# Attention scores by 64-row halves of the matmul array, three products instead of four

## The chip, the cores and the metric

The kernel runs on one core of a Trainium2 chip. Its engines work side by side, each through its own list of instructions in order: TensorE (PE; its weight loads are listed apart as PEld), VectorE (DVE), ScalarE (ACT), GpSimd (POOL) and SyncE (SP), which here issues nearly all DMA transfers. The metric is the device time of one execution, in microseconds; the time of a kernel is the median of several runs. TensorE's clock has two levels, 1.2 and 2.4 GHz; the profile shows the granted one as 0.50 and 1.00.

## The reference

Four batches, eight heads, 576 positions, head dimension 64. Attention with a bias that depends on position alone, then a mixing along the sequence, then a two-layer network over 512 channels, all in float32:

```
scores = q @ k.T / 8 + bias(i, j)         # bias: 1 -> 32 -> 8 heads, from log1p(|i-j|) / log1p(max(i,1))
attn   = exp(scores - max); attn /= sum + 1e-9
x      = (attn @ v)  as [4, 576, 512]
h      = x.T @ U @ V                       # along the sequence, rank 32
u      = x + h.T
out    = u + relu(u @ w_ch1) @ w_ch2       # 512 -> 2048 -> 512
```

## The kernel before

Attention goes by pairs of heads: 16 pairs (`p`), each in nine slots (`s`). 576 query rows are four blocks of 128 and 64 left over. Slot 0 does the leftover rows of both heads of the pair in one tile of 128; slots 1 to 8 do the four blocks of the two heads in turn. A slot's scores are a 128x576 tile in two PSUM banks of 288 keys each (`ps`, line 323).

To keep float32 accuracy with the faster `float32r` type, q and k are split into a high part and a rest. `raw` holds a pair's q and k, loaded twice so that both 64-row halves of the partitions hold the same 64 dimensions. `prep_ops` (lines 145 to 170) writes `hi` (high parts; for q the upper 64 partitions are then overwritten with the rest, line 163) and `lo` (the rest of k). A matmul over 128 partitions with q's high part and rest stacked as weights, against k's high part on both halves, gives two of the products; the same weights against k's rest give the other two. So each half of the keys takes two matmuls of 128x288 (line 343), four per slot, with a weight load each. In slot 0 each head's leftover queries stand beside zeros (64 columns of padding), and the two heads are added up: eight matmuls.

For pair 0 `prep_ops` runs early on ACT and DVE, inside the loop that builds the bias; for the others it runs on POOL, in slots 2 to 5 of the pair before. `raw` has one buffer: the load of pair p+2 (`load_pair`, lines 132 to 138, issued in slot 7) waits until POOL has finished with pair p+1. `hi` and `lo` have two.

The order of the work is the order in which the code issues it. `slot` (line 513) issues a slot's scores first, then transposes (lines 411, 419, 428, 465, 467) of tiles that earlier slots have finished, the exponentials on ACT, and in slots 2 and 8 the products with v (line 447, tile `o`). DVE adds the bias and takes the row maximum (line 345) straight from PSUM. So PE goes, in most slots, from scores to transposes and on to the next scores. Transposes and scores work on the whole array (128x128); `o` works on 128x64 column tiles, two of them side by side; `mt` (line 486), once per batch, on 128x32 column tiles, its last part on 64x32. Between 345 us and the end there is only the network (lines 592 and 615), which the change doesn't touch except for the width of a tile.

Of the kernel before, what the change touches and what calls it, by code (L numbers as in the profile page):

```python
# [8 lines left out]
F32 = mybir.dt.float32  # L9
F32R = mybir.dt.float32r  # L10
# [4 lines left out]
ALU = mybir.AluOpType  # L15
# [3 lines left out]
B, H, S, D = 4, 8, 576, 64  # L19
HP = H // 2  # L20
DM = H * D
# [4 lines left out]
P = 128  # L26
HALF = S // 2
LEFT = S - 4 * P
K0 = 2 * S + LEFT
QKW = 2 * K0  # L30

LINE = 16
NTAB = 2 * S - 1
# [15 lines left out]
def kernel(  # L49
# [13 lines left out]
):  # L63
    nc = tc.nc
    mm = nc.tensor.matmul

    def halves(ap):
        return ap.rearrange("p (a b) -> p a b", a=2)
# [6 lines left out]
    p0 = ExitStack()  # L75
# [9 lines left out]
    qkp = ctx.enter_context(tc.tile_pool(name="qkp", bufs=2, side="left"))  # L85
# [27 lines left out]
    rawp = p1.enter_context(tc.tile_pool(name="rawp", bufs=1, side="left"))  # L113
# [5 lines left out]
    qk_ops = {}  # L119
    v_t = {}  # L120

    def pair_loads(p):

        b, hp = divmod(p, HP)

        def part(lo, a, e):
            if p not in qk_ops:
                qk_ops[p] = rawp.tile([P, QKW], F32, tag="raw", name="raw")
            nc.sync.dma_start(out=qk_ops[p][lo : lo + D, a:e], in_=qk[b, hp, :, a:e])

        return [lambda: part(0, 0, QKW), lambda: part(D, LEFT, QKW), lambda: part(D, 0, LEFT)]

    def load_pair(p):
        b, hp = divmod(p, HP)
        raw = rawp.tile([P, QKW], F32, tag="raw", name="raw")
        nc.sync.dma_start(out=raw[0:D], in_=qk[b, hp])
        nc.sync.dma_start(out=raw[D:P], in_=qk[b, hp])
        qk_ops[p] = raw

    def load_v(p):  # L140
        b, hp = divmod(p, HP)
# [3 lines left out]
    def prep_ops(p, early=False):  # L145


        hi = qkp.tile([P, QKW], F32R, tag="hi", name="hi")
        lo = qkp.tile([P, K0 + 2 * LINE], F32R, tag="lo", name="lo")[:, LINE : LINE + K0]
# [11 lines left out]
        def low(out, a, e, p0):  # L161
            eng = nc.vector if early else nc.gpsimd
            eng.tensor_tensor(out=out, in0=raw[p0:P, a:e], in1=hi[p0:P, a:e].bitcast(F32), op=ALU.subtract)  # L163

        return [
            lambda: high(0, K0),
            lambda: low(hi[D:P, 0:K0], 0, K0, D),
            lambda: high(K0, QKW),
            lambda: low(lo, K0, QKW, 0),
        ]  # L170

# [53 lines left out]
    for g in range(4):  # L225
        r = slice(g * HID, (g + 1) * HID)
# [91 lines left out]
    def scores(p, s):  # L318
        d = pair[p]
        hi, lo = qk_ops[p]  # L320
        hp = p % HP
        st = d["st"]
        ps = psum("s", [P, 2, 512], "sc")
        if s == 0:
            terms = [(4 * P, 0), (S, S + LEFT)]
            dst = pmp.tile([P, S], F32, tag="praw", name="praw")
            d["praw"] = dst
        else:
            c, hd = divmod(s - 1, 2)
            if hd == 0:  # L330
                terms = [(c * P, 0)]
                d["P"][c] = pp.tile([P, 2 * S], F32, tag="p", name="p")
                dst = d["P"][c][:, 0:S]
            else:
                terms = [(S + 2 * LEFT + c * P, S)]
                dst = d["P"][c][:, S : 2 * S]
        for a in range(2):
            n = 2 * len(terms)
            i = 0
            for q0, k0 in terms:  # L340
                k1 = k0 + a * HALF
                for kk in (hi[:, K0 + k1 : K0 + k1 + HALF], lo[:, k1 : k1 + HALF]):
                    mm(ps[:, a, 0:HALF], lhsT=hi[:, q0 : q0 + P], rhs=kk, start=(i == 0), stop=(i == n - 1))  # L343
                    i += 1
        nc.vector.tensor_tensor_reduce(  # L345
            out=halves(dst),
            in0=ps[:, :, 0:HALF],
            in1=halves(bias[hp][:, s * S : (s + 1) * S]),
            scale=-0.125,
            scalar=3.0e38,  # L350
            op0=ALU.add,
            op1=ALU.min,
            accum_out=st[:, s : s + 1],
        )
        d["dst"] = dst
# [189 lines left out]

    KD = DM // P
    TB = 256
    NB = NT // TB  # L550
    TT = TB // P
    NG = 4
# [2 lines left out]
    UT = KD * TB  # L555

    acc, uth, utl, wq, hh, hl = {}, {}, {}, {}, {}, {}
# [22 lines left out]
    def mlp1(n):  # L580

        g, j = divmod(n, NB)
        st = {}

        def step(f):
            if f == 0:
                st["ps"] = psum("s", [P, FG, TB], "ph")
            i = 0
            for k in range(KD):
                wh, wl = (w[:, k, f * P : (f + 1) * P] for w in wq[g][0:2])  # L590
                for w, u in ((wh, uth[j]), (wh, utl[j]), (wl, uth[j])):
                    mm(st["ps"][:, f, :], lhsT=w, rhs=u[:, k, :], start=(i == 0), stop=(i == 3 * KD - 1))  # L592
                    i += 1
            if f == FG - 1:
                t = qkp.tile([P, QKW], F32R, tag="hi", name="hh")
# [94 lines left out]
    for i in range(len(order) + 2):  # L690
        if i < len(order):
            bias_hid(order[i])
        if i >= 2:
            bias_mm(order[i - 2])
            bias_out(order[i - 2])
        if i == 9:
            loads += bias_loads(4, 0)
        if i >= 16 and (i - 16) % 8 == 0:
            loads += bias_loads((i - 16) // 8, 0)
        if i in (28, 30):  # L700
            loads += bias_loads({28: 4, 30: 0}[i], 1)
# [107 lines left out]
    t = [qkp.tile([P, K0 + 2 * LINE], F32R, tag="lo", name="ut") for _ in range(2)]  # L809
# [140 lines left out]
```

## Time and profile before

| what | value |
|---|---|
| median of 3 runs | 775.45 us (773.51 to 777.46) |
| the profiled execution | 771.65 us |
| its span, first to last instruction | 769.8 us |
| PE busy | 740.3 us, 96% of the span |
| DVE, ACT, POOL busy | 56%, 46%, 30% |
| chain that ended last | PE 74%, POOL 7%, DMA 6%, DVE 6%, ACT 4% |
| TensorE clock | 1.00 but for two stretches of 3.4 us |

The page shows three stages: until about 56 us the bias is built (DVE and ACT full, DMA near full), until about 345 us attention runs with the conversion of weights in the background, and then the network to the end. A matmul's listed time includes its way through the array, so consecutive ones overlap: how long PE is taken by one is read from the distance between starts, not from the listed time.

### The profile page before, as it was taken

The page shows a single profiled execution, that of the slowest core. Times are in us where ns is not written, and L with a number is a line of the kernel's source. Part 1 is how long each engine was busy: PE and PEld are TensorE (multiplying, and loading weights), DVE is VectorE, ACT ScalarE, POOL GpSimd, SP SyncE. Part 2 cuts the span into 40 slices and gives each one's busy share as a digit, 9 for nine tenths or more (in the row PEclk, how much of TensorE's full clock was granted, in tenths as well). Part 3 has the DMA queues.
Part 4 walks back from the last instruction along what each step waited for, and adds up shares of the span by engine and source line. Part 5 has one row for each costly group of instructions (what it writes and reads, how often), then busy time and mean ns, then how long its engine had stood idle before and what let it go on. Part 6 is the DMA issues. An engine that isn't in the chain of part 4 may idle for free.

```text
span 769.8 us, 13411 instructions
## 1 busy us (share of the span) xinstructions
PE 740.3 (96%) x5132; PEld 612.0 (80%) x5132; DVE 431.4 (56%) x953; ACT 354.4 (46%) x827; POOL 234.3 (30%) x222
## 2 busy tenths in 40 slices
PE   6888899999999999999999999999999999999998
PEld 4326787778768777779789889988998999899986
DVE  7984478868867876662448734762247722221222
ACT  6995677678767676863025513431114410111010
POOL 0004446656664566710015502540015500000000
PEclk9999999999999999999999999999999999999999
DMA  6898994564455547530153301320002200001111
GB/s 200 262 340 265 241 274 112 138 165 124 124 171 138 123 97 209 160 129 2 38 189 110 96 1 42 96 83 1 1 27 84 69 1 1 1 29 55 55 42 69
DMA packets 39423, 83.97 MB, mean 109 GB/s; under 512 B 6976, under 2 KB 9536, under 8 KB 37312
## 3 DMA queue, kind: packets, MB, share of 16 engines
q1 hardware_dynamic: 39120, 82.86, 37.1%
q8 instruction: 41, 0.67, 0.4%
q10 hardware_dynamic: 240, 0.26, 0.1%
q14 instruction: 22, 0.18, 0.1%
HBM read 60.67 MB, written 22.43 MB: 108 GB/s over the span
## 4 chain that ended last, share of the span: by engine, by line
PE 74%; POOL 7%; DMA 6%; DVE 6%; ACT 4%; issue 2%; SPq 1%; DVEq 0%; POOLq 0%; ACTq 0%
PE po L615 24%; PE ph L592 24%; PE o L447 8%; PE sc L343 7%; PE tb L411 5%; DMA raw<-in_qk_dram 4%; DVE ring L260 2%; POOL lo L163 2%; POOL hi L163 2%; POOL hi L157 2%; PE mt L486 1%; DVE wt L207 1%; ACT p L364 1%; PE bs L270 1%; PE tm L419 1%
## 5 line engine op out<-in xcount | busy, mean ns | idle before, releaser
L597 ACT ACTIVATE hh<-ph 128x1024 fp32r<-128x1024 f32 x36 | 36.9, 1026 | 207.6 <-PE ph L592 207.6
L598 DVE SCALAR_TENSOR_TENSOR hh<-ph,hh 128x1024 fp32r<-128x1024 f32 x36 | 44.1, 1224 | 141.2 <-ACT hh L597 141.2
L212 POOL TENSOR_TENSOR wy<-wt,wy 128x256 int32<-128x256 int32 (+1 forms) x68 | 50.2, 739 | 218.7 <-DVE wt L207 198.0
L364 ACT ACTIVATE p<-p,st 128x576 f32<-128x576 f32 x128 | 100.0, 782 | 34.9 <-DVE st L345 34.8
L345 DVE CUSTOM_DVE_ANT_0 p<-sc,bias 128x576 f32<-128x576 f32 x128 | 95.9, 749 | 33.3 <-PE sc L343 26.2
L343 PE MATMUL sc<-hi 128*128 128x288 f32 x320 | 101.8, 334 | 2.0 <-DVE st L345 2.0
L615 PE MATMUL po<-w2q,hh 128*128 128x512 f32 x432 | 101.7, 390 | 1.8 <-DVE acc L618 1.8
L615 PE MATMUL po<-wq,hh 128*128 128x512 f32 x432 | 103.2, 395 | 0.0
L343 PE MATMUL sc<-lo,hi 128*128 128x288 f32 x320 | 90.7, 299 | 3.9 <-POOL lo L163 3.8
L615 PEld LDWEIGHTS po<-w2q,hh 128*128 128x128 f32 x432 | 79.9, 188 | 18.1 <-issue 2.0
L592 PE MATMUL ph<-ut,w1q 128*128 128x256 f32 x768 | 94.2, 280 | 0.0
L615 PEld LDWEIGHTS po<-wq,hh 128*128 128x128 f32 x432 | 80.1, 188 | 17.6
L592 PEld LDWEIGHTS ph<-ut,w1q 128*128 128x128 f32 x768 | 92.1, 188 | 2.1 <-issue 1.2
L447 PE MATMUL o<-pt,v 128*64 128x320 f32 (+1 forms) x640 | 91.2, 412 | 0.9 <-ACT pt L391 0.9
L592 PEld LDWEIGHTS ph<-ut,wq 128*128 128x128 f32 x768 | 90.3, 188 | 1.4
L592 PE MATMUL ph<-ut,wq 128*128 128x256 f32 x768 | 90.6, 277 | 0.0
L618 DVE TENSOR_TENSOR acc<-po,acc 128x512 f32<-128x512 f32 x72 | 49.6, 690 | 73.1 <-PE po L615 73.1
L411 PE MATMUL tb<-ident,p 128*128 128x128 f32 x512 | 77.8, 275 | 3.9 <-DVE x_sb L393 2.5
L343 PEld LDWEIGHTS sc<-hi 128*128 128x128 f32 x320 | 60.9, 190 | 19.2 <-issue 11.6
L447 PEld LDWEIGHTS o<-pt,v 128*64 128x64 f32 x640 | 45.2, 136 | 35.9 <-ACT pt L391 5.5
L157 POOL TENSOR_SCALAR hi<-raw 128x1216 fp32r<-128x1216 f32 x30 | 36.9, 1231 | 105.7 <-DMA raw<-in_qk_dram 90.3
L411 PEld LDWEIGHTS tb<-ident,p 128*128 128x128 f32 x512 | 61.9, 141 | 5.9 <-ACT p L364 2.5
(94 smaller groups left out, 1037.0 us busy)
## 6 DMA issues: line engine op xcount, KB each, us to landing
raw<-in_qk_dram SPq DMA_DIRECT2D x31, 608.0 KB, 7.6
wraw<-in_w_ch_dram SPq DMA_DIRECT2D x64, 256.0 KB, 2.7
bias_dram<-ring SPq DMA_DIRECT2D x26, 295.5 KB, 4.2
v<-in_vp_dram SPq DMA_DIRECT2D x16, 320.0 KB, 8.2
bias<-bias_dram SPq DMA_DIRECT2D x16, 288.0 KB, 4.6
acc<-u_dram SPq DMA_DIRECT2D x18, 256.0 KB, 4.8
out_dram<-acc SPq DMA_DIRECT2D x18, 256.0 KB, 2.0
bias<-bias_dram SPq DMA_DIRECT2D x16, 256.0 KB, 4.7
```

The costliest lines, as they stand in the source:

```text
L157: nc.gpsimd.tensor_scalar(out=hi[:, a:e], in0=raw[:, a:e], scalar1=1.0, scalar2=0.0, op0=ALU.mult, op1=ALU.add)
L212: nc.gpsimd.tensor_tensor(out=st["y"], in0=st["t"], in1=st["y"], op=ALU.add)
L343: mm(ps[:, a, 0:HALF], lhsT=hi[:, q0 : q0 + P], rhs=kk, start=(i == 0), stop=(i == n - 1))
L345: nc.vector.tensor_tensor_reduce(out=halves(dst), in0=ps[:, :, 0:HALF], in1=halves(bias[hp][:, s * S : (s + 1) * S]), scale=-0.125, scalar ...
L364: nc.scalar.activation(out=dst, in_=dst, func=AF.Exp, bias=st[:, s : s + 1], scale=-1.0, accum_out=st[:, 10 + s : 11 + s])
L411: nc.tensor.transpose(bank[:, kb, :], src[:, b0 + kb * P : b0 + (kb + 1) * P], ident)
L447: mm(o[hd * D : (hd + 1) * D, 0:n], lhsT=v[:, vb * D : (vb + 1) * D], rhs=pt[:, pb, :], start=(j == 0), stop=(j == 4),)
L592: mm(st["ps"][:, f, :], lhsT=w, rhs=u[:, k, :], start=(i == 0), stop=(i == 3 * KD - 1))
L597: nc.scalar.activation(out=hh[n], in_=st["ps"], func=AF.Relu)
L598: nc.vector.scalar_tensor_tensor(out=hl[n], in0=st["ps"], scalar=0.0, in1=hh[n].bitcast(F32), op0=ALU.max, op1=ALU.subtract)
L615: mm(ps, lhsT=h, rhs=w, start=(m == 0), stop=(m == 3 * FG - 1))
L618: nc.vector.tensor_tensor(out=a, in0=ps, in1=a, op=ALU.add)
```

## The change

Scores are now made with weights of 64 rows. The lower 64 partitions hold q and the first 288 keys, the upper 64 hold q again and the last 288 keys. High part and rest lie in two tiles of the same layout, `hi` and `lo`, and three products are made: high by high, high by rest, rest by high; rest by rest is left out. Each product is two matmuls, one on each 64-row half of the array, into the two PSUM banks. A slot takes six matmuls of 64x128 weights by 288 columns. Slot 0 makes all 128 leftover rows against the second head's keys, and then the first 64 rows again, against the first head's keys, with 64x64 weights: twelve matmuls; the zero padding is no longer read. A pair's load is six transfers of 917 KB together, formerly two of 1,245 KB together; pair 1's, formerly three with the last at step 32 of the bias loop, has its four key pieces at steps 32 to 35. Conversions are four of 128x896.

```diff
-QKW = 2 * K0
+KA = HALF
+KB = LEFT + HALF
+QQ = 2 * S
+QKW = QQ + KA + KB
...
+        def q(lo):
+            nc.sync.dma_start(
+                out=raw(lo, 0, QQ).rearrange("d (t n) -> d t n", t=2),
+                in_=src[:, 0 : 2 * (S + LEFT)].rearrange("d (t n) -> d t n", t=2)[:, :, 0:S],
+            )
+        def k(lo, to, n, a):
+            nc.sync.dma_start(out=raw(lo, to, n), in_=src[:, a : a + n])
+        return [
+            lambda: q(0),
+            lambda: q(D),
+            lambda: k(0, QQ, KA, K0),
+            lambda: k(D, QQ, KA, K0 + KA),
+            lambda: k(0, QQ + KA, KB, K0 + S),
+            lambda: k(D, QQ + KA, KB, 2 * K0 - KB),
+        ]
...
-            lambda: high(0, K0),
-            lambda: low(hi[D:P, 0:K0], 0, K0, D),
-            lambda: high(K0, QKW),
-            lambda: low(lo, K0, QKW, 0),
+        m = QKW // 2
+        return [lambda: high(0, m), lambda: low(0, m), lambda: high(m, QKW), lambda: low(m, QKW)]
...
-            terms = [(4 * P, 0), (S, S + LEFT)]
+            parts = [(4 * P, P, QQ + KA + LEFT), (4 * P, D, QQ)]
...
-        for a in range(2):
-            n = 2 * len(terms)
-            i = 0
-            for q0, k0 in terms:
-                k1 = k0 + a * HALF
-                for kk in (hi[:, K0 + k1 : K0 + k1 + HALF], lo[:, k1 : k1 + HALF]):
-                    mm(ps[:, a, 0:HALF], lhsT=hi[:, q0 : q0 + P], rhs=kk, start=(i == 0), stop=(i == n - 1))
-                    i += 1
+        terms = ((hi, hi), (hi, lo), (lo, hi))
+        for q0, n, k0 in parts:
+            for i, (q, k) in enumerate(terms):
+                for a in range(2):
+                    r = slice(a * D, (a + 1) * D)
+                    mm(
+                        ps[0:n, a, 0:HALF], lhsT=q[r, q0 : q0 + n], rhs=k[r, k0 : k0 + HALF],
+                        start=(i == 0), stop=(i == len(terms) - 1),
+                    )
...
-        if i in (14, 18, 32):
+        if i in (14, 18, 32, 33, 34, 35):
```

PE's list in pair 1, from the transposes of slot 0 to those of slot 1. Before (`sc` scores, `tb` and `ti` transposes):

```order
L411 MATMUL tb<-ident,p 128x128 x4
L343 MATMUL sc<-hi 128x288
L343 MATMUL sc<-lo,hi 128x288
L343 MATMUL sc<-hi 128x288
L343 MATMUL sc<-lo,hi 128x288
L411 MATMUL tb<-ident,p 128x128 x4
L428 MATMUL ti<-ident,p 128x128 x2
```

The same place in the list after the change:

```order
L429 MATMUL tb<-ident,p 128x128 x4
L359 MATMUL sc<-hi 128x288 x2
L359 MATMUL sc<-lo,hi 128x288 x2
L359 MATMUL sc<-hi,lo 128x288 x2
L429 MATMUL tb<-ident,p 128x128 x4
L446 MATMUL ti<-ident,p 128x128 x2
```

Four score matmuls of the whole array became three twos of 64-row weights (the order gives the rows of the output, 128), between the same transposes.

PE's list from the product with v at the end of pair 0 to the first transposes of pair 1, slot 0 of pair 1 between them. Before:

```order
L447 MATMUL o<-pt,v 64x320 x10
L343 MATMUL sc<-hi 128x288
L343 MATMUL sc<-lo,hi 128x288
L343 MATMUL sc<-hi 128x288
L343 MATMUL sc<-lo,hi 128x288
L343 MATMUL sc<-hi 128x288
L343 MATMUL sc<-lo,hi 128x288
L343 MATMUL sc<-hi 128x288
L343 MATMUL sc<-lo,hi 128x288
L411 MATMUL tb<-ident,p 128x128 x4
```

The same place in the list after the change:

```order
L465 MATMUL o<-pt,v 64x320 x10
L359 MATMUL sc<-hi 128x288 x2
L359 MATMUL sc<-lo,hi 128x288 x2
L359 MATMUL sc<-hi,lo 128x288 x2
L359 MATMUL sc<-hi 64x288 x2
L359 MATMUL sc<-lo,hi 64x288 x2
L359 MATMUL sc<-hi,lo 64x288 x2
L429 MATMUL tb<-ident,p 128x128 x4
```

Eight matmuls became two groups of six, the second with 64 columns of weights.

POOL's list for one pair, the leftover rows' scaling (`pm`) and the conversion of the next pair. Before:

```order
L384 TENSOR_SCALAR pm<-praw,st 128x576
L384 TENSOR_SCALAR pm<-praw,st 128x64
L157 TENSOR_SCALAR hi<-raw 128x1216
L163 TENSOR_TENSOR hi<-raw,hi 64x1216
L157 TENSOR_SCALAR hi<-raw 128x1216
L163 TENSOR_TENSOR lo<-raw,hi 128x1216
```

The same place in the list after the change:

```order
L402 TENSOR_SCALAR pm<-praw,st 128x576
L402 TENSOR_SCALAR pm<-praw,st 128x64
L178 TENSOR_SCALAR hi<-raw 128x896
L184 TENSOR_TENSOR lo<-raw,hi 128x896
L178 TENSOR_SCALAR hi<-raw 128x896
L184 TENSOR_TENSOR lo<-raw,hi 128x896
```

The number of instructions stays, each conversion is over 896 columns, and all are over 128 partitions.

## Rows read from the trace of the kernel before

**Rows 1.** The page, its engines (part 1) and its chain (part 4).

```profile
PE 740.3 (96%) x5132; PEld 612.0 (80%) x5132; DVE 431.4 (56%) x953; ACT 354.4 (46%) x827; POOL 234.3 (30%) x222
...
PE 74%; POOL 7%; DMA 6%; DVE 6%; ACT 4%; issue 2%; SPq 1%; DVEq 0%; POOLq 0%; ACTq 0%
```

**Rows 2.** The view by stretches: length, then busy us (instructions) per engine, clock, DMA.

```profile
30.00:56.00 26.00, 21.09 (x176) 7.26 (x174) 24.60 (x75) 25.14 (x62) 0.00 (x0) 0.93 0.98 333
...
89.20:92.60 3.40, 3.40 (x17) 3.37 (x16) 0.99 (x4) 1.07 (x2) 0.00 (x0) 0.50 0.85 184
...
125.00:175.00 50.00, 49.19 (x361) 38.84 (x361) 38.22 (x101) 36.24 (x93) 28.78 (x25) 1.00 0.60 154
345.00:770.00 425.00, 418.97 (x2732) 376.59 (x2728) 176.79 (x282) 99.01 (x204) 70.80 (x96) 1.00 0.15 49
```

**Rows 3.** Waits of PE from 56 to 345 us: us, times, longest.

```profile
PE sc L343 <- POOL lo L163: 3.8, 3, 2.2
...
PE tx L465 <- DVE w2q L568: 0.2, 1, 0.2
```

**Rows 4.** PE in order of time, 253.5 to 255.9: start, us, line, form, [idle before].

```profile
253.28 0.44 PE L447 MATMUL o<-pt,v 128*64 128x320 f32 x2
253.65 0.40 PE L343 MATMUL sc<-hi 128*128 128x288 f32 x1
253.88 0.29 PE L343 MATMUL sc<-lo,hi 128*128 128x288 f32 x1
...
254.67 0.30 PE L343 MATMUL sc<-lo,hi 128*128 128x288 f32 x1
254.81 0.60 PE L411 MATMUL tb<-ident,p 128*128 128x128 f32 x4
...
255.38 0.30 PE L343 MATMUL sc<-lo,hi 128*128 128x288 f32 x1
...
255.80 0.33 PE L411 MATMUL tb<-ident,p 128*128 128x128 f32 x1
```

**Rows 5.** PE's weight loads (PEld) of the same stretch.

```profile
253.64 0.19 PEld L343 LDWEIGHTS sc<-hi 128*128 128x128 f32 x1 [0.49 <-issue]
...
255.13 0.19 PEld L343 LDWEIGHTS sc<-hi 128*128 128x128 f32 x1
```

**Rows 6.** PE in order of time, 250 to 254, the groups ahead of those.

```profile
250.27 0.60 PE L411 MATMUL tb<-ident,p 128*128 128x128 f32 x4
250.80 2.91 PE L447 MATMUL o<-pt,v 128*64 128x320 f32 x20
```

**Rows 7.** PEld, 141.55 to 144.0, the mixing product's two tile shapes.

```profile
141.59 0.16 PEld L486 LDWEIGHTS mt<-x_sb,u_sb 128*32 128x32 f32 x8 [0.49 <-DVE x_sb L470]
142.59 0.14 PEld L486 LDWEIGHTS mt<-x_sb,u_sb 64*32 64x32 f32 x2 [0.84 <-issue]
```

**Rows 8.** PE, 114.5 to 115.5, transposes of two tile shapes.

```profile
114.65 0.38 PE L465 MATMUL tx<-ident,ot 128*128 128x128 f32 x2
114.87 0.27 PE L467 MATMUL tx<-ident,ot 128*64 128x128 f32 x1
114.97 0.60 PE L411 MATMUL tb<-ident,p 128*128 128x128 f32 x4
```

**Rows 9.** POOL's groups by form: busy us, mean ns, idle before.

```profile
L163 POOL TENSOR_TENSOR lo<-raw,hi 128x1216 fp32r<-128x1216 f32 x15 | 42.3, 2817 | 1.1
L163 POOL TENSOR_TENSOR hi<-raw,hi 64x1216 fp32r<-64x1216 f32 x15 | 42.0, 2801 | 1.2
L157 POOL TENSOR_SCALAR hi<-raw 128x1216 fp32r<-128x1216 f32 x30 | 36.9, 1231 | 105.7 <-DMA raw<-in_qk_dram 90.3 <-PE sc L343 7.0 <-PE tb L411 6.9
```

**Rows 10.** PE, 86.2 to 89.8, pair 2's second matmul.

```profile
88.86 0.40 PE L343 MATMUL sc<-lo,hi 128*128 128x288 f32 x1 [2.16 <-POOL lo L163]
```

**Rows 11.** DMA issues: KB each, median us to landing.

```profile
raw<-in_qk_dram SPq DMA_DIRECT2D x31, 608.0 KB, 7.6
```

**Rows 12.** SP's list, 86 to 91 us, the first load after that wait.

```profile
88.83 0.48 SPq L136 DMA_DIRECT2D raw<-in_qk_dram  x1
```

More of the change, by code (lines that the diff above doesn't have):

```diff
@@ L65 @@
     mm = nc.tensor.matmul
+    KD = DM // P
+    TB = 256
     def halves(ap):
@@ L124, in pair_loads, with raw @@
         b, hp = divmod(p, HP)
-        def part(lo, a, e):
+        src = qk[b, hp]
+        def raw(lo, to, n):
             if p not in qk_ops:
                 qk_ops[p] = rawp.tile([P, QKW], F32, tag="raw", name="raw")
-            nc.sync.dma_start(out=qk_ops[p][lo : lo + D, a:e], in_=qk[b, hp, :, a:e])
-        return [lambda: part(0, 0, QKW), lambda: part(D, LEFT, QKW), lambda: part(D, 0, LEFT)]
-    def load_pair(p):
[L134 to L138, printed above, removed]
+            return qk_ops[p][lo : lo + D, to : to + n]
+        def q(lo):
[13 more added lines that the diff above has]
+        ]
+    def load_pair(p):
+        for o in pair_loads(p):
+            o()
     def load_v(p):
@@ L145, in prep_ops @@
     def prep_ops(p, early=False):
-        hi = qkp.tile([P, QKW], F32R, tag="hi", name="hi")
-        lo = qkp.tile([P, K0 + 2 * LINE], F32R, tag="lo", name="lo")[:, LINE : LINE + K0]
+        hi = qkp.tile([P, 2 * KD * TB], F32R, tag="hi", name="hi")
+        lo = qkp.tile([P, QKW], F32R, tag="lo", name="lo")
         raw = qk_ops[p]
@@ L159, in high, with low @@
                 )
-        def low(out, a, e, p0):
+        def low(a, e):
             eng = nc.vector if early else nc.gpsimd
-            eng.tensor_tensor(out=out, in0=raw[p0:P, a:e], in1=hi[p0:P, a:e].bitcast(F32), op=ALU.subtract)
-        return [
-            lambda: high(0, K0),
-            lambda: low(hi[D:P, 0:K0], 0, K0, D),
-            lambda: high(K0, QKW),
-            lambda: low(lo, K0, QKW, 0),
-        ]
+            eng.tensor_tensor(out=lo[:, a:e], in0=raw[:, a:e], in1=hi[:, a:e].bitcast(F32), op=ALU.subtract)
+        m = QKW // 2
+        return [lambda: high(0, m), lambda: low(0, m), lambda: high(m, QKW), lambda: low(m, QKW)]
     def conv_ops(src, n, finish):
@@ L330, in scores @@
             if hd == 0:
-                terms = [(c * P, 0)]
+                parts = [(c * P, P, QQ)]
                 d["P"][c] = pp.tile([P, 2 * S], F32, tag="p", name="p")
@@ L334, in scores @@
             else:
-                terms = [(S + 2 * LEFT + c * P, S)]
+                parts = [(S + LEFT + c * P, P, QQ + KA)]
                 dst = d["P"][c][:, S : 2 * S]
-        for a in range(2):
-            n = 2 * len(terms)
-            i = 0
-            for q0, k0 in terms:
-                k1 = k0 + a * HALF
-                for kk in (hi[:, K0 + k1 : K0 + k1 + HALF], lo[:, k1 : k1 + HALF]):
-                    mm(ps[:, a, 0:HALF], lhsT=hi[:, q0 : q0 + P], rhs=kk, start=(i == 0), stop=(i == n - 1))
-                    i += 1
+        terms = ((hi, hi), (hi, lo), (lo, hi))
[7 more added lines that the diff above has]
+                    )
         nc.vector.tensor_tensor_reduce(
@@ L543, in slot @@
             av(p, 0)
-    KD = DM // P
-    TB = 256
     NB = NT // TB
@@ L594, in step @@
             if f == FG - 1:
-                t = qkp.tile([P, QKW], F32R, tag="hi", name="hh")
+                t = qkp.tile([P, 2 * UT], F32R, tag="hi", name="hh")
                 hh[n], hl[n] = (t[:, a * UT : (a + 1) * UT].rearrange("p (f t) -> p f t", f=FG) for a in range(2))
@@ L808 @@
     uth[1], utl[1], uth[2], utl[2], uth[3] = big_views(t, [(LINE, None)] + [(UT, KD)] * 5)
-    t = [qkp.tile([P, K0 + 2 * LINE], F32R, tag="lo", name="ut") for _ in range(2)]
+    t = [qkp.tile([P, QKW], F32R, tag="lo", name="ut") for _ in range(2)]
     utl[3], uth[4] = (x[:, LINE : LINE + UT].rearrange("p (k f) -> p k f", k=KD) for x in t)
```

## The prediction

> **What bounds the kernel now.** I read the page's engine part first: PE is busy 96% of the span, the next engine 56%, and the chain that ended last lies on PE for 74% [rows 1]. A busy PE is not yet a bound, since overlapping matmuls count as busy, so I went on to the stretches. In the network (345 us to the end) PE is busy 418.97 of 425 us; nothing the change does reaches there. In attention, 125 to 175 us stands for the rest: PE 49.19 of 50, DVE 38.22, ACT 36.24, POOL 28.78. Only the bias stage is different: at 30 to 56 us DVE and ACT are busy 24.60 and 25.14 of 26 and the DMA engines 0.98, PE less [rows 2]. The list of waits agrees: from 56 to 345 us PE waited for another engine 11.4 us in all (eight rows, the first and the last shown), and 3.8 of them for POOL's conversion of the next pair [rows 3]. So in attention PE's own time decides, and any microsecond put on it or taken off counts nearly in full; at most 11.4 us can come from waits that go away. The chain's 7% on POOL and 6% on DMA say that load and conversion are nearly as late as PE, not that they hold it up for long.
>
> **What a group of scores costs now.** Between the first and the last matmul rows of slot 3, the starts 253.88 and 254.67 are six matmuls apart: 0.132 us each. Coming from transposes costs nothing more: from the first of four transposes (254.81) to the second score matmul (255.38) is 0.57 = 4 x 0.109 + 0.132; the weight load at 255.13 began ahead of its turn and shows no idle time. Nor does going back to transposes: 254.67 to 254.81 is 0.14 [rows 4, 5]. So a usual slot holds PE for 4 x 0.132 = 0.53 us and slot 0 for 1.06.
>
> **Turns saved.** If the two halves of the array work side by side, a two of matmuls takes one turn of 0.132. The rows show it for column tiles: the last two `o` matmuls stand as one row of 0.44, both started at 253.28, and 20 such matmuls last only 2.91 [rows 4, 6]. For row halves no row shows it; I take it over. Then slots 1 to 8 go from four turns to three and slot 0 from eight to six: 10 turns a pair, 160 in all, 21.1 us saved.
>
> **Boundaries added.** Every change of the array's shape shows a price in this trace. (1) Whole array to `o`: the four transposes begin at 250.27, their turns end at 250.27 + 4 x 0.109 = 250.71, `o` begins at 250.80: 0.09 empty [rows 6]. (2) `o` to scores: nine twos lie between 250.80 and 253.28, so the last has its turn until about 253.28 + 0.27 = 253.55; the scores' weight load begins only at 253.64, with idle time put to "issue": again 0.09, and then the load itself is exposed, as the second matmul comes 0.23 after the first (253.65, 253.88) and not 0.13: 0.10 more [rows 4, 5]. (3) Rows alone: `mt` goes from 128x32 to 64x32 tiles, and that load waits 0.84 us although nothing it needs is late [rows 7]. A load into a transpose exposes less: the transposes that start at 255.80, whose load was not ahead of time, have a first row of 0.33 [rows 4] against 0.27 [rows 8]: 0.06. So I price entering a group of 64-row scores from transposes at 0.09 + 0.11 = 0.20 and leaving it at 0.09 + 0.06 = 0.15. Both stand on PE, with nothing beside them.
>
> The Trainium skill has this as a rule: "TensorEngine Tiling (Array Packing)", section "Key Properties", says that changing the tiling mode drains TensorE, while going from one tile to another in the same mode does not. The rows at (1) to (3) agree with it; those of [rows 8] do not, on their face, and make a rival below.
>
> **The sum on PE, per pair.** Slots 1, 4, 5, 6, 7 and 8 stand between transposes: -0.13 + 0.35 = +0.22 each, 1.32. Slot 2 is followed by `o`, where the boundary exists already: -0.13 + 0.20 = +0.07. Slot 3 follows `o`: -0.13 + 0.15 = +0.02. Slot 0 follows `o` too, saves two turns, changes from 64x128 to 64x64 weights in its middle (0.09 + 0.06 for half as many columns) and goes on to transposes: -0.26 + 0.15 + 0.15 = +0.04. Together +1.45, for 16 pairs 23.2; pair 0's slots 0 to 2 stand between bias matmuls of another shape, in the stage that DVE and ACT bound, and drop out: about -0.3. So +22.9 us.
>
> **What is given back.** POOL's conversion of a pair is 2 x 1.23 + 2 x 2.81 = 8.1 us [rows 9]; over 896 of 1216 columns 6.0 (the op over 64 partitions took as long as that over 128, so the wider one costs nothing). The load falls from 1,245 to 917 KB, at 7.6 us to landing per transfer of 608 KB [rows 11]. Load and conversion are thus some 3 to 4 us earlier per pair while PE is 1.4 later: I take POOL's 3.8 us of waits as gone. The longest, 2.16 us at 88.86 [rows 10], is followed by 3.4 us at half clock [rows 2], which held some 1.7 us of work at full clock; I give back 1.5. Of the other 7.6 us, waits for DVE and ACT, a slower PE lets part vanish: between none and all, I take half, 3.8. Sum 9.1. Four more transfers per pair, at 0.48 us each [rows 12], cost SP about 2 us; SP issues in slot 7 for a pair whose conversion starts two slots into the next, and that cover of several slots is shorter only where the DMA engines are near full (until 95 us). There pair 1's key pieces are issued up to three steps later than the last piece before, but the first half of its conversion, all of q, can be done by then, so half of POOL's work is no longer behind that landing. If the cover fails, a wait of the size of the old 2.16 stays: the lower give-back, 5.
>
> **Forecast.** +22.9 - 9.1 = +13.8 on the profiled 771.65: 785.5. The median of the runs is 3.8 above that execution, so 789 in its terms. Bounds of the likeliest case: turns of 0.120 (288 columns at one a cycle of 2.4 GHz) give 480 x 0.012 = 5.8 less, all 11.4 us of waits gone 3.8 less; the give-back of 5, 4 more. Its own range is 780 to 797.
>
> **Rivals.** (A) No boundary between the whole array and row halves. For it: one transpose in a 128x64 shape stands between whole-array ones at 114.87, 0.11 after the second of the two that begin at 114.65, and the next follow at 114.97 without a gap [rows 8]; and all changes with a price but one also change the number type. Against it: that one, `mt`, changes rows alone. Then 21.1 us are saved, POOL's waits and the half clock give 5, and DVE and ACT, busy three quarters of the time, return a part as new waits, say 5 to 10: 775.45 - 19 = 756 (748 to 764). (B) A boundary of 0.09 each way, but with loads pulled ahead, since the other half's weights don't stand in the way: usual slots -0.13 + 0.18 = +0.05, per pair 0.3 - 0.04 - 0.04 - 0.08 = +0.14, 2 us in all, less 9 given back: 768. Against it is the load at 253.64, which began only after the gap. (C) The halves don't run side by side. If only their weight loads queue up, a two takes 2 x 0.11 = 0.21: 480 x 0.08 = 38 more, 827; it decides as soon as the second load of a two has to wait for the first. If the matmuls themselves do, 480 x 0.132 = 63 more, 852. For it: no 64-row twos anywhere in the trace; against it the `o` matmuls. The change would then not do what it says. "TensorE: Matmul & The Clock Gate", section "LDWEIGHTS (loading the stationary operand)" of the Trainium skill, puts a load at its columns over 1.2 GHz whatever the rows: 107 ns by that rule, an estimate for each of the two halves, and the exposed 0.10 agrees.
>
> **How the numbers follow.** The forecast 0.58, A 0.20, B 0.10, C 0.12. The range of 750 to 806 takes in the forecast with its edges, B and most of A; C and the better end of A, under 0.2 together, stay outside. What a measurement of this kernel tells from no change is about 0.5%, 4 us. Faster: A, most of B and a corner of the forecast, 0.28. Same: 0.07. Slower: 0.65.
>
> **What would show it.** In the trace after: two score matmuls starting within 0.01 us of each other (else C); the next two 0.13 later; the first weight load of a group 0.09 after the last transposes' turn, with idle time put to "issue", and a first two that takes 0.1 longer (without these, A or B); the distance between the first transposes of neighbouring slots 0.2 longer; PE's wait for POOL `lo` gone and no half clock near 89 us; conversions of 0.9 and 2.1 us on POOL. A time under 771 makes the boundary price wrong, one over 806 the side-by-side assumption.

## The result: 0.6% slower, and the profile after

| | before | changed |
|---|---|---|
| median, 20 runs each | 773.8 us | 777.97 us |
| lowest to highest | 769.78 to 777.71 | 777.10 to 779.79 |
| ratio | 1 | 1.0057 (95%: 1.0042 to 1.0071) |
| profiled execution's span | 769.8 us | 776.0 us |
| start of the first to start of the last product with v that closes a pair (after slot 8) | 279.8 us | 288.0 us |
| from there to the end | 425.7 us | 423.8 us |

The changed kernel is slower by 4.2 us; 789 had been forecast. Times of before lie far apart, those of the changed kernel close together; the profiled execution of before was one of its fast ones.

First the page of the changed kernel, the engines of part 1 and from part 6 the load of q (as [rows 1] and [rows 11]; the keys' pieces are rows of their own):

```profile
PE 751.6 (97%) x5452; PEld 593.7 (77%) x5452; DVE 437.2 (56%) x953; ACT 355.2 (46%) x827; POOL 204.2 (26%) x222
...
raw<-in_qk_dram SPq DMA_DIRECT2D x32, 288.0 KB, 4.6
```

The view by stretches, as in [rows 2]:

```profile
30.00:56.00 26.00, 20.01 (x180) 6.88 (x182) 25.79 (x71) 24.44 (x59) 3.14 (x2) 0.93 0.97 318
125.00:175.00 50.00, 49.63 (x395) 33.80 (x393) 37.01 (x95) 35.08 (x91) 25.48 (x25) 1.00 0.38 110
352.00:776.00 424.00, 419.50 (x2739) 376.65 (x2737) 177.52 (x283) 99.90 (x206) 70.84 (x96) 1.00 0.15 50
```

PE has more work in the same 50 us (49.19 busy before, 49.63 now), POOL and the DMA engines less. The bias stage and the network are nearly as they were.

What PE does around the scores, in order of time, in the changed kernel (as [rows 4]):

```profile
251.72 0.40 PE L359 MATMUL sc<-hi 64*128 64x288 f32 x2
251.96 0.29 PE L359 MATMUL sc<-lo,hi 64*128 64x288 f32 x2
252.09 0.29 PE L359 MATMUL sc<-hi,lo 64*128 64x288 f32 x2
252.32 0.65 PE L429 MATMUL tb<-ident,p 128*128 128x128 f32 x4
252.81 0.38 PE L446 MATMUL ti<-ident,p 128*128 128x128 f32 x2
253.03 0.27 PE L449 MATMUL ti<-ident,pm 128*128 128x128 f32 x1
253.23 0.40 PE L359 MATMUL sc<-hi 64*128 64x288 f32 x2
```

PE again, in slot 0 of another pair, where the weights narrow to 64 columns:

```profile
180.58 0.40 PE L359 MATMUL sc<-hi 64*128 64x288 f32 x2
180.82 0.30 PE L359 MATMUL sc<-lo,hi 64*128 64x288 f32 x2
180.96 0.29 PE L359 MATMUL sc<-hi,lo 64*128 64x288 f32 x2
181.09 0.29 PE L359 MATMUL sc<-hi 64*64 64x288 f32 x2
181.22 0.29 PE L359 MATMUL sc<-lo,hi 64*64 64x288 f32 x2
181.36 0.29 PE L359 MATMUL sc<-hi,lo 64*64 64x288 f32 x2
181.58 0.66 PE L429 MATMUL tb<-ident,p 128*128 128x128 f32 x4
```

PE's weight loads beside the first of these blocks, at its two boundaries (as [rows 5]):

```profile
252.31 0.42 PEld L429 LDWEIGHTS tb<-ident,p 128*128 128x128 f32 x4 [0.16 <-issue]
...
253.23 0.18 PEld L359 LDWEIGHTS sc<-hi 64*128 64x128 f32 x2 [0.17 <-issue]
```

A two stands as one row: its matmuls start 3 to 4 ns apart, and the next two follows 0.13 later (251.96 to 252.09). So the halves run side by side. The transpose at 253.03 has its turn until 253.14, the scores' load begins at 253.23: 0.09 empty. The second two comes 0.24 after the first and not 0.13: 0.10 of exposed load. On the way back the last turn ends at 252.09 + 0.13 = 252.22, the transposes begin at 252.32, and from the first four to `ti` it is 0.49 = 4 x 0.109 + 0.055. So entering costs 0.20 and leaving 0.15, as priced. But the change from 64x128 to 64x64 weights within slot 0 costs nothing: 180.96 to 181.09 is a plain turn.

### The profile page after: what moved, and what is told of

It is laid out like the page before. It is cut to its first block, busy times and chain, and to the rows that moved or that the text cites. A ratio compares the mean times of both kernels' runs of the same rounds, so it can differ in the third digit from the quotient of the medians.

```text
span 776.0 us, 14159 instructions
## 1 busy us (share of the span) xinstructions
PE 751.6 (97%) x5452; PEld 593.7 (77%) x5452; DVE 437.2 (56%) x953; ACT 355.2 (46%) x827; POOL 204.2 (26%) x222
## 4 chain that ended last, share of the span: by engine, by line
PE 78%; ACT 8%; DVE 8%; DMA 3%; issue 2%; POOL 1%; SPq 1%; ACTq 0%; DVEq 0%; POOLq 0%
PE po L631 24%; PE ph L608 23%; PE o L465 8%; PE sc L359 8%; PE tb L429 6%; PE bs L287 3%; DVE wt L218 2%; ACT p L382 2%; ACT pt L409 1%; DVE p L363 1%; PE tm L437 1%; PE mt L504 1%; DVE wt L212 1%; PE tx L483 1%; ACT ring L275 1%
## 5 line engine op out<-in xcount | busy, mean ns | idle before, releaser
L631 PEld LDWEIGHTS po<-w2q,hh 128*128 128x128 f32 x432 | 79.9, 188 | 16.7 <-issue 0.6
L465 PE MATMUL o<-pt,v 128*64 128x320 f32 (+1 forms) x640 | 88.7, 411 | 0.6 <-ACT pt L409 0.6
L429 PE MATMUL tb<-ident,p 128*128 128x128 f32 x512 | 82.2, 283 | 3.4 <-DVE x_sb L411 1.8
L465 PEld LDWEIGHTS o<-pt,v 128*64 128x64 f32 x640 | 50.8, 136 | 27.6 <-issue 3.0
L429 PEld LDWEIGHTS tb<-ident,p 128*128 128x128 f32 x512 | 55.0, 140 | 20.9 <-issue 11.7
L409 ACT COPY pt<-tb 128x512 f32<-128x512 f32 x88 | 50.9, 579 | 30.4 <-PE tb L429 30.2
L359 PE MATMUL sc<-hi 64*128 64x288 f32 (+1 forms) x320 | 62.4, 386 | 1.9 <-DVE st L363 1.8
L184 POOL TENSOR_TENSOR lo<-raw,hi 128x896 fp32r<-128x896 f32 x30 | 63.2, 2108 | 2.2
L359 PEld LDWEIGHTS sc<-hi 64*128 64x128 f32 (+1 forms) x320 | 29.0, 178 | 40.0 <-issue 32.1
## 6 DMA issues: line engine op xcount, KB each, us to landing
raw<-in_qk_dram SPq DMA_DIRECT2D x32, 288.0 KB, 4.6
bias<-bias_dram SPq DMA_DIRECT2D x16, 288.0 KB, 4.4
```

Source lines behind the costliest of these rows:

```text
L184: eng.tensor_tensor(out=lo[:, a:e], in0=raw[:, a:e], in1=hi[:, a:e].bitcast(F32), op=ALU.subtract)
L359: mm(ps[0:n, a, 0:HALF], lhsT=q[r, q0 : q0 + n], rhs=k[r, k0 : k0 + HALF], start=(i == 0), stop=(i == len(terms) - 1),)
L409: nc.scalar.copy(out=out, in_=in_)
L429: nc.tensor.transpose(bank[:, kb, :], src[:, b0 + kb * P : b0 + (kb + 1) * P], ident)
L465: mm(o[hd * D : (hd + 1) * D, 0:n], lhsT=v[:, vb * D : (vb + 1) * D], rhs=pt[:, pb, :], start=(j == 0), stop=(j == 4),)
L631: mm(ps, lhsT=h, rhs=w, start=(m == 0), stop=(m == 3 * FG - 1))
```

## Where PE waited, before and after

Waits of PE from 56 us to the end of attention in the changed kernel, as [rows 3]; all its rows:

```profile
PE tb L429 <- DVE x_sb L411: 1.8, 2, 1.0
PE sc L359 <- DVE st L363: 1.8, 1, 1.8
PE tm L437 <- DVE x_sb L411: 1.6, 5, 0.3
PE tb L429 <- DVE pt L411: 0.8, 1, 0.8
PE o L465 <- ACT pt L409: 0.6, 1, 0.6
```

POOL's `lo` is gone from the list, as forecast. The list of PE's weight loads, which the prediction does not use, says more. In before, from 56 to 345 us, its two longest waits for another engine:

```profile
PEld sc L343 <- POOL lo L163: 6.3, 7, 2.4
PEld o L447 <- ACT pt L391: 5.5, 12, 1.2
```

In the changed kernel, to 352 us, `lo` is gone from this list too, and of the second row is left:

```profile
PEld o L465 <- ACT pt L409: 1.0, 1, 1.0
```

A matmul's wait can stand on the row of the weight load ahead of it and not on its own. The second of before's two lines is a wait in nearly every pair: the product with v after slot 2 goes on to its second half of weights only when ACT has copied `pt`. In before, PE's row of one such product, and the load's row from the other list:

```profile
183.93 2.95 PE L447 MATMUL o<-pt,v 128*64 128x256 f32 x20
```

```profile
184.51 1.92 PEld L447 LDWEIGHTS o<-pt,v 128*64 128x64 f32 x18 [0.39 <-ACT pt L391]
```

The same product in the changed kernel:

```profile
184.16 2.69 PE L465 MATMUL o<-pt,v 128*64 128x256 f32 x20
```

And in a run with four products, told of below:

```profile
194.66 2.42 PE L465 MATMUL o<-pt,v 128*64 128x256 f32 x20
```

Slots 1 and 2 take PE 0.21 and 0.06 longer in the changed kernel than in before, and two more turns, 0.26, with four products; each time the product gets shorter by as much. ACT's copy ends when it ends, PE arrives later and waits less. Over the first 15 such products, each from its start to the start of what follows on PE, it is 42.1 us in before and 39.3 in the changed kernel: 2.8 us given back.

## A VectorE operation that lasts as long as its neighbour

DVE's rows of one slot 2 of the changed kernel, in order of time:

```profile
185.56 0.88 DVE L212 TENSOR_SCALAR wt<-wt 128x256 f32<-128x256 f32 x1 [0.52 <-ACT wt L206]
186.47 2.15 DVE L218 TENSOR_SCALAR wt<-wt 128x256 int32<-128x256 int32 x1
188.55 0.74 DVE L363 CUSTOM_DVE_ANT_0 p<-sc,bias 128x576 f32<-128x576 f32 x1
```

POOL's rows of the same stretch:

```profile
185.35 0.94 POOL L178 TENSOR_SCALAR hi<-raw 128x896 fp32r<-128x896 f32 x1
186.38 2.10 POOL L184 TENSOR_TENSOR lo<-raw,hi 128x896 fp32r<-128x896 f32 x1
```

The clamp and the shift of the weights' conversion (`wt`) take 0.29 us elsewhere. Here they end at 186.44 and 188.62, 0.15 after POOL's operations beside them (186.29 and 188.48). The bias addition of the next scores, which PE had finished by about 187.5, starts at 188.55, as the stall ends. By DVE's rows of attention, such operations are longer than 0.30 us by 10.6 us in all in before (13 operations) and 18.8 us in the changed kernel (17): POOL's conversion now begins, in ordinary pairs, 7.6 us after the product with v that closes a pair, in before mostly 10 to 12 us after it, and the weights' conversion that follows slot 2 meets it in nearly every pair.

The next step of the weights' conversion on DVE, the join (line 207; 224 in the changed kernel), is held up in the same way, but only in before. Its group from 56 to 350 us (columns as in [rows 9]), and the longest one:

```profile
L207 DVE SCALAR_TENSOR_TENSOR wt<-wraw,sgn,wt 128x256 int32<-128x256 int32 x18 | 12.4, 689 | 0.3
```

```profile
249.57 2.60 DVE L207 SCALAR_TENSOR_TENSOR wt<-wraw,sgn,wt 128x256 int32<-128x256 int32 x1
```

POOL's row beside it:

```profile
249.10 2.78 POOL L163 TENSOR_TENSOR lo<-raw,hi 128x1216 fp32r<-128x1216 f32 x1
```

The same group in the changed kernel:

```profile
L224 DVE SCALAR_TENSOR_TENSOR wt<-wraw,sgn,wt 128x256 int32<-128x256 int32 x18 | 8.3, 459 | 0.3
```

A join takes 0.43 to 0.49 us with POOL idle. Six of before's are longer, by 5.4 us over 0.46 each. So the stalls of DVE are 16.0 us in before and 18.8 in the changed kernel. Below, "stalls" alone are those of clamp and shift; the join's are named.

Pairs (distance between the starts of neighbouring products with v after slot 8; those with mixing, the first two and the last left out) are 16.5 to 18.3 us long in before, 17.4 to 18.2 in the changed kernel. Theory 1: these stalls hold PE up, and are part of the difference. Theory 2: only PE's own turns and boundaries decide.

## Experiments: is a turn worth a turn

The changed kernel with a fourth product, and with two.

```diff
-        terms = ((hi, hi), (hi, lo), (lo, hi))
+        terms = ((hi, hi), (hi, lo), (lo, hi), (lo, lo))   # four_products
+        terms = ((hi, hi), (hi, lo))                       # two_products
```

> The changed kernel with the fourth product, rest by rest, put back: one two of matmuls more per group, two in slot 0. 160 turns of 0.131 us are 21.0 us. Theory (PE's turns in attention count in full): 778.0 + 21 less 1 or 2 of waits that vanish, 795 to 799. Rival (DVE and ACT set the pace in part, so that PE's time is half hidden): 786 to 791. Rival (the two halves would not really run side by side): +42 us, 820.

> The changed kernel without the third product (rest of q by high part of k is left out): 160 turns of 0.131 us fewer, 21.0 us. If PE's time counts in full: 757. The fourth product cost 15.4 of its 21.0 us, so DVE and ACT are close behind, and in this direction more of it must come back as waits: 762 to 768, waits of PE in attention up by 6 us or more.

Measured 793.25 (ratio to before 1.0256, 1.0234 to 1.0279) and 769.31 (0.9954, 0.9937 to 0.9970): by the ratios +15.4 and -8.0 us against the changed kernel, where each step is 160 turns of 0.131, 21 us. Up, 4.2 of the missing 5.6 us are the product with v: 39.3 to 35.1 us in 15 products. Down, PE runs into what the others deliver: the same products rise by 3.9, and DVE's stalls stay (18.7 us). The first lies between its two ranges, the second 1.3 us above its own; that the halves take turns (820) is out.

## Experiments: the lighter load and conversion

Before without the conversion of the keys' rest, the high part read in its place (POOL's conversion of a pair 5.2 us instead of 8.1; in the changed kernel it is 6.1); the changed kernel with the load and conversion of before's size; before with one load of q and k where two are.

```diff
# before_short_prep (before)
-            lambda: low(lo, K0, QKW, 0),
+            lambda: None,
...
-                for kk in (hi[:, K0 + k1 : K0 + k1 + HALF], lo[:, k1 : k1 + HALF]):
+                for kk in (hi[:, K0 + k1 : K0 + k1 + HALF], hi[:, K0 + k1 : K0 + k1 + HALF]):
# old_amounts (changed kernel): 640 more columns loaded and converted
...
+            lambda: [k(D, QQ + KA, KB, 2 * K0 - KB), k(0, QKW, 640, K0), k(D, QKW, 640, K0)],
...
+            lambda: [high(0, 640), high(0, m)],
+            lambda: [low(0, 640), low(0, m)],
# before_half_load (before)
...
+        if not raw1:
+            nc.sync.dma_start(out=raw[D:P], in_=qk[b, hp])
```

> The kernel before without the conversion of k's rest (POOL 2.8 us less per pair, raw free that much earlier); the second matmul of each half reads k's high part again, so rest of k is left out of the products while all matmuls stay. Theory: the chain of load and conversion costs the kernel before some 4 to 8 us (waits for POOL of 3.8 us, a half-clock stretch of 1.7 us, and more in its slower runs): 766 to 770, and its runs lie closer together than 769.8 to 777.7. Rival: those waits only move to DVE and ACT, the give-back came from PE being slower: 773 to 774 with the same spread.

> The changed kernel with the load and the conversion of a pair made as large as in the kernel before: two more transfers of 64x640 per pair (1,245 KB in all) into columns that nothing reads, and 640 more columns of high part and of rest, written twice. The score matmuls are untouched. Theory A: the lighter chain of load and conversion is the larger part of what was given back, so it costs 3 to 6 us again: 781 to 784. Theory B: with PE slower per pair the old chain would be early enough anyway, and what was given back are short waits for DVE and ACT: 777 to 779.

> The kernel before with only one of the two copies of q and k loaded from pair 2 on (622 KB instead of 1,245; the upper 64 partitions keep pair 1's values), all conversions and matmuls as before. Theory A (the chain of load and conversion costs the kernel before 4 to 6 us, and shortening the conversion alone let the load take its place): 767 to 769, runs within 3 us of each other. Theory B (the chain is only as late as PE itself): 771 to 773, spread as before.

Measured 770.44 (0.9975, 0.9957 to 0.9993), 778.06 (1.0070, 1.0047 to 1.0093) and 781.59 (1.0123, 1.0100 to 1.0146). The first, 1.9 us under before, lies between its two theories, and its runs are no closer together (766.95 to 774.68): the wait for `lo` became one for `hi` behind the load (3.9 us in two waits). The second is as slow as the changed kernel, as theory B has it, but with stalls of 9.4 us, and 5.0 of the join, where that had 18.8 and none: either the smaller amounts give the changed kernel nothing, or the longer conversion eats what fewer stalls give; this run alone can't tell. What the shorter conversion gives before is in the last section of experiments. The third lies 8.6 us above the higher of its two ranges: with the load out of the way, conversions started earlier (7.8 us after the product with v that closes a pair), beside DVE's `wt`, whose stalls rose to 28.6 us. PE's waits from 56 to 345 us in that run, the longest row:

```profile
PE sc L346 <- DVE st L348: 8.7, 9, 1.6
```

It is in this miss that the stalls show most.

## Experiments: half as many boundaries

If boundaries are the price, scores of two slots in a row pay once for both. The control is the same in before, where there are none.

```diff
...
-        if new:
+        if new and (p == 0 and s < 5 or s == 0):
             scores(p, s)
+        elif new and s % 2:
+            scores(p, s)
+            scores(p, s + 1)
...
# the act_first versions also: ACT, not DVE, copies the first head's transposes
-            tr(p, c, hd, "a" if p % HP == 1 and 2 < s < 6 else "da"[hd])
+            tr(p, c, hd, "a" if p % HP == 1 and 2 < s < 6 else "ad"[hd])
```

> The changed kernel with the scores of slots 1 and 2, 3 and 4, 5 and 6, 7 and 8 issued back to back, ahead of the transposes of both slots (pair 0 from slot 5 on). Theory: each entry into a 64-row group costs PE 0.20 us and each exit into transposes 0.145, fully on the path. Four entries and three exits fewer per pair are 1.235 us, some 19 us in all; two tiles waiting in PSUM at once bring back 2 to 8 us as waits for DVE. So 778.0 - 19 + 5 = 764 (760 to 769). Rival 1: a good part of the boundary time lies beside waits for DVE and ACT that would be there anyway: 772 to 778. Rival 2: with two score buffers the second group of a pair always waits for DVE's row maximum: 778 or more.

> Control: the kernel before with the same regrouping. It has no boundaries between scores and transposes, so the theory expects nothing saved: 774 with up to 6 us of new waits, 773 to 780. Rival: regrouping helps by itself (longer runs of one kind of matmul, later transposes that wait less): 765 to 770.

> The regrouped kernel with the two evacuations of a group's transposes swapped: the first on ACT, which has nothing to do until DVE has made the row maximum, the second on DVE behind its two row maxima. Theory: the 4.6 us that PE waited for DVE's evacuations before the ti transposes go, 767 to 769, faster than both kernels. Rival: another PSUM wait takes their place, 771 to 773.

> The kernel before (four products, whole-array scores) with the two edits of the fastest version so far: scores of two slots issued together, and ScalarE taking the first head's transposes out of PSUM instead of VectorE. Control: is the gain of 16.7 us over the changed kernel due to half as many boundaries, or to the order of the evacuations? In before there is no boundary at the scores, so regrouping can give nothing there (alone it cost 8 us). Boundaries decide: 771 to 781, 10 to 20 us slower than the same two edits on the changed kernel. Evacuation order decides: 758 to 766, as fast or faster.

| | on before | on the changed kernel |
|---|---|---|
| grouped | 780.93 (1.0105, 1.0087 to 1.0123) | 772.07 (0.9993, 0.9980 to 1.0006) |
| grouped, ACT first | 772.85 (0.9995, 0.9981 to 1.0009) | **761.29** (0.9855, 0.9832 to 0.9877) |

Regrouping costs before 8.1 us (transposes and scores wait for DVE, 3.5 and 2.7 us) and gives the changed kernel 4.9; with the order of copies set right, the 64-row scores win by 10.8 us (0.9855 against 0.9995), as the control's theory of the boundaries has it. The other forecasts missed: regrouping alone gave 4.9 us where 14 were expected (rival 1's range holds the time), its control came out just above its range, and the version with ACT first 6 us below its own. In the regrouped changed kernel DVE's copy was late. PE's waits from 56 to 345 us there, the longest row:

```profile
PE ti L446 <- DVE pt L411: 4.6, 11, 0.4
```

With ACT first this row is gone; PE's longest waits in the same stretch:

```profile
PE sc L359 <- DVE st L363: 2.2, 1, 2.2
PE tb L429 <- DVE x_sb L411: 1.8, 2, 0.9
PE tm L437 <- DVE x_sb L411: 0.3, 1, 0.3
```

Its pairs are mostly 16.5 us long, and the stalls, the join's with them, 0.4 us in all, in the regrouped kernel without this edit 0.2: here the conversions came to lie apart. Before with the same two edits keeps 15.4 us of them. So this version beats both kernels, by boundaries and stalls together; how much of the 4.9 and of the 10.8 us is the stalls', no run separates.

## Experiments: the stalls

The weights' conversion after slot 2 goes to slot 7, which then has two, in the changed kernel, in before, and in the changed kernel with two products.

```diff
-    conv_at = (0, 1, 2, 6, 7, 8)
+    conv_at = (0, 1, 6, 7, 7, 8)
...
-                background(int(s in conv_at and (p, s) >= CONV_FROM))
+                background(conv_at.count(s) if (p, s) >= CONV_FROM else 0)
```

> The changed kernel with one edit: of the six weight conversions of a pair, the one that follows slot 2 follows slot 7 instead, which then has two. Theory 1 (VectorE's clamps of the weights last as long as the operation on GpSimd beside them, and this holds PE up): the stalls of slot 2, most of 18.8 us, go, the pairs of 18.2 us become 17.0 to 17.5, and the time falls by 3 to 7 us to 771 to 775. Theory 2 (PE's own boundaries and turns decide, the stalls lie beside PE's work): within 1.5 us of the changed kernel, 776.5 to 779.5. Two conversions in slot 7 may make a new wait of VectorE there; then under 2 us come back.

> The kernel before with the same edit (the conversion of slot 2 in slot 7). Its stalls were 10.6 us in eleven operations. Theory 1: three to five pairs of 18.4 us become 16.6, so 3 to 6 us off: 767 to 770, and the spread of its runs (769.8 to 777.7) narrows. Theory 2: within 1.5 us of before.

> The changed kernel with the conversion of slot 2 in slot 7, and only two of the three products in the scores (the third, lo of the queries with hi of the keys, is left out). 160 twos of turns less, 21.1 us on PE. With the stalls there only 8.7 us of them came off the time. Theory 1 (what was missing had turned into stalls of VectorE): against the changed kernel with that edit alone, 13 to 20 us off. Theory 2 (attention without the third product is bound by VectorE and ScalarE whatever the stalls): 6 to 11 us off.

Measured 774.26 (1.0015, 1.0004 to 1.0025), 777.27 (1.0047, 1.0030 to 1.0064) and 762.65 (0.9856, 0.9840 to 0.9873). In the changed kernel the stalls went. DVE's two `wt` groups from 56 to 350 us in the changed kernel (columns as in [rows 9]):

```profile
L218 DVE TENSOR_SCALAR wt<-wt 128x256 int32<-128x256 int32 x18 | 18.9, 1051 | 0.6
L212 DVE TENSOR_SCALAR wt<-wt 128x256 f32<-128x256 f32 x18 | 9.8, 547 | 3.7 <-ACT wt L206 3.7
```

The same groups with the conversion in slot 7:

```profile
L218 DVE TENSOR_SCALAR wt<-wt 128x256 int32<-128x256 int32 x18 | 5.3, 294 | 0.6
L212 DVE TENSOR_SCALAR wt<-wt 128x256 f32<-128x256 f32 x18 | 5.2, 289 | 0.3
```

The same work in another slot: 18.8 us of DVE's time back, 3.2 us of the kernel's (1.0057 to 1.0015), and every ordinary pair is now 17.4 us long; the join has no stalls here either. Theory 1 holds at its lower edge: most of the stalls lay beside PE's work. In before the edit missed: its longer conversion met the clamps in other slots, 15.5 us of stalls and 1.3 of the join, and the time rose. With two products 12.3 us come off by the ratios (11.6 by the medians; 8.0 with the stalls), between the two theories' ranges: the stalls were one part of what was missing, the product with v that waits for ACT another (2.2 us of it).

## Experiments: the account

Last, clamp and shift taken out on both sides, and then the wait for POOL too. In the conversions that run beside attention the clamp and the shift are left out, and the join stays; the third kernel is before with that and without the conversion of the keys' rest, as in before_short_prep.

```diff
...
-            groups += [[size, low], [clamp, shift], [join, add]]
+            groups += [[size, low], [] if lean else [clamp, shift], [join, add]]
```

> The kernel before without clamp and shift in the 20 weight conversions that run beside attention (those of the rows u and v and of the first set of network weights are then wrong values; the later sets are converted in full). No VectorE operation of the kind that stalled is left in attention. Theory 1 (stalls were a good part of the time before): pairs of 18.4 us fall to 16.6 where POOL is not late; 3 to 6 us off, 767 to 770. Theory 2 (the stalls lie beside PE's work): within 1.5 us of before, since the waits for GpSimd's lo stay.

> The changed kernel without clamp and shift in the same 20 conversions. Theory 1: as with the conversion of slot 2 moved, pairs of 17.4 us throughout, 772.5 to 775. Theory 2: within 1.5 us of the changed kernel. Against the kernel before with the same cut, theory 1 has 5 to 8 us more, theory 2 some 4.

> The kernel before without these clamps and shifts and with GpSimd converting 896 of 1,216 columns of a pair, as in the changed kernel (the rest of the keys' low parts is left unconverted). Neither stalls nor, by theory 1, waits for lo are left: pairs of 16.5 us throughout, 762 to 766, and the changed kernel with the same cut 8 to 12 us slower: PE's 16.7 us less the 2.8 that the loads of o waited for ScalarE in before, and what is left of DVE. If waits for the load of raw come in their place, as in the short conversion alone, 766 to 769.

| step | ratio to before | us of this step |
|---|---|---|
| before, no clamps | 0.9997 (0.9982 to 1.0013) | -0.2 |
| and POOL's conversion short | 0.9920 (0.9903 to 0.9938) | -6.0 |
| and scores by 64-row halves: the changed kernel, no clamps | 1.0019 (1.0005 to 1.0033) | +7.7 |
| and the clamps: the changed kernel | 1.0057 (1.0042 to 1.0071) | +2.9 |

Each step is a difference of ratios by 773.3 us, uncertain by 1.2 to 1.8 us. In the first run theory 2 held: before was no faster. But its stalls were not gone. The join now met POOL's operations in eight of 20 conversions, for 8.1 us in all (5.4 in before), and POOL's `lo` stayed late (5.4 us on the loads' list). The join's group from 56 to 350 us in that run:

```profile
L207 DVE SCALAR_TENSOR_TENSOR wt<-wraw,sgn,wt 128x256 int32<-128x256 int32 x18 | 14.9, 830 | 0.3
```

So what the stalls cost before stays open. In the third kernel 2.4 us of the join's are left, so its 6.0 us are the wait for POOL and 5.7 us of stalls together. It came 1 us above the expected 762 to 766; the other range, up to 769, was for waits behind the load, and none stands in its lists. The changed kernel without clamps has no stalls left. It is as fast as theory 1 had it, 7.6 us behind the third kernel (8 to 12 expected), but only 1.7 behind before without clamps, less than either theory had. From the third kernel to it, ordinary pairs go from mostly 16.5 to 16.7 us to 17.4, and the product with v falls from 43.5 to 39.4 us (15 products). The pair's 0.8 and that product's 0.27 make 1.1 of the 1.2 that PE's rows give for the boundaries less the turns (the sum is in the next section). Over all pairs that sum is 18.9 us, the time rose by 7.7: of the 11.2 us between them 4.1 are the product with v, up to 3.7 the end of the kernel, and the rest stays open.

Why the end came 2 to 4 us sooner after the last product that closes a pair where attention was slower (423.8 and 424.0 us against 425.7 and 427.7, each in the profiled execution) is mostly shown. PE's wait for DVE's `acc` fell from 1.8 to 0.4 us in the changed kernel, and from 2.0 to 0.6 from the third kernel to the changed kernel without clamps. In the third kernel that wait was followed by 3.4 us at half clock, which held 1.7 us of work at full clock. Its stretch, as in [rows 2]:

```profile
427.70:431.10 3.40, 3.40 (x10) 2.62 (x9) 3.24 (x7) 2.61 (x8) 2.20 (x3) 0.50 0.44 145
```

The changed kernels have the full clock there. That makes 1.4 of 1.9 and 3.1 of 3.7 us; what else shrank stays open.

## Why the prediction was wrong

The direction was right: slower, 0.65. The size was not: 15.2 us above the 20-run median of before were forecast, 4.2 measured.

- **Turns saved, boundaries added.** Right in their parts. Twos side by side, 0.13 to the next, 0.09 empty each way, 0.10 and 0.055 of exposed loads all stand in the trace after. A usual slot costs +0.21 (forecast 0.22), slot 2 +0.06 (0.07), slot 3 +0.02 as forecast; medians, from the start of the last matmul ahead of the scores to that of the second behind them. The eight score matmuls from 253.65 in [rows 4] are slot 0's and not slot 3's; the 0.132 does not depend on it.
- **Slot 0, the term that was wrong on PE.** +0.04 was forecast with 0.15 for an inner switch of shape. It costs nothing, so the slot gives -0.14. Over all, the sum on PE is +1.2 per pair and 18.9 us, not 1.45 and 22.9: 4.0 us too much, most of it here. [Rows 8] had shown it: the transpose of 128x64 between whole ones lost no time. I had read the price from `mt` [rows 7], whose wait may have been another. What fits the rows shown: going to or from tiles that lie side by side in the array, in rows or in columns (`o`), costs; narrower weights in the same place do not. No run tests this rule by itself.
- **What is given back, the step that failed.** 9.1 us were forecast, net 14.7 came back (18.9 less 4.2). POOL's `lo` was taken at 3.8 from PE's list [rows 3], where the loads' list had 6.3; the shorter conversion gave 1.9 by itself, and 6.0, part of the join's stalls with it, once the clamps were out. "Any microsecond put on it counts nearly in full; at most 11.4 can come from waits that go away" was wrong in the same way: the loads of `o` behind ACT's copy, 5.5 us in before, stand in no row that the prediction uses, and gave back 2.8 (4.1 without clamps). The end of the kernel gave 1.9 more (profiled executions). A further turn counts 15.4 of 21.0. What is left of the 14.7 is not assigned to a wait.
- **What nobody forecast.** Stalls of DVE: without them the changed kernel stands at 1.0015 to 1.0019, 2.9 to 3.2 us lower. So most of the 4.2 us goes away with them, and that the direction came out clear of the noise is in part luck. Before has stalls too, 16.0 us; what they cost it stays open, since no run takes them out of before and changes nothing else.
- **The base.** I added 3.8 us for the distance of a profiled execution to a median of three runs. The changed kernel's profiled execution (778.02) is its median; the 20-run median of before is 773.8, 1.65 lower than the three runs'. So 4.0 + 5.6 + 1.65 make the 11 us. The upper edge of the range, 797, has no term behind it: the give-back of 5 makes 793.
- Rivals: C fell with the twos side by side, A and B with the 0.20 and 0.15 at the boundaries, though A's sign, the narrow transpose without a price, holds for narrower weights. The half clock near 89 us went as forecast; conversions take 0.96 and 2.11 us (forecast 0.9 and 2.1).

## What to carry to other kernels

Price a change of shape by whether tiles come to lie side by side in the array, not by whether weights get narrower, and put work of one shape in a row: the same 64-row scores lose by 0.6% one slot at a time and win by 1.4% two at a time with the copies in the right order, where the stalls differ too. Read the waits of the weight loads beside those of the matmuls before saying what a microsecond on PE is worth: before's matmuls showed 3.8 us for POOL's `lo` and 0.9 for ACT's `pt`, its loads 6.3 and 5.5. And when an edit shifts the rhythm, look for operations whose duration has changed though they have not.

## What was not expected of the hardware

DVE's TENSOR_SCALAR on float32 or int32 in SBUF, 128x256, takes 0.29 us alone and up to 2.87 (before with the short conversion) beside a GpSimd operation that started before it; it ends mostly 0.15 us after that one ends, whatever its own work (0.88 beside 0.94, 2.15 beside 2.10). The join, a SCALAR_TENSOR_TENSOR of 0.43 to 0.49 us, takes up to 3.05 (before, regrouped) and in the instance shown ends 0.28 after GpSimd's. The bias addition, which reads scores from PSUM, was not stretched (0.74 to 0.76 us beside the same operations). The Trainium skill states it in "SBUF — State Buffer", section "Who interferes with whom": VectorE in a mode that uses two ports shares one pair with GpSimd, and the one that issues second blocks fully until the first is done. The trace agrees in the blocking and in the order: POOL's operations start 0.21 and 0.09 before DVE's. The mode itself no trace here shows.
